# Chunkwise mLSTM cell into a leaky-ReLU feed-forward: one row order of w_in on both partition halves, quarter 2 converted earlier, first feed-forward chunk by token halves

## The chip, the cores and the metric

The kernel runs on one core of one Trainium2 chip. A core has five engines that run side by side, each working through its own instructions in order: TensorE (PE in the profile; PEld is its weight load), VectorE (DVE), ScalarE (ACT), GpSimd (POOL) and SyncE (SP), which here only issues transfers. The metric is the device time of one execution in microseconds. A change is called faster, the same or slower by comparing medians of interleaved runs.

## The reference

Inputs: q, k, v and o_gate of shape (4, 8, 768, 40), i_gate and f_gate of shape (4, 8, 768), and two weight matrices, w_in (320, 2048) and w_out (2048, 320). The weights are float64 in memory, the rest float32. Two blocks follow one another:

```python
for t in range(S):                       # S = 768, per batch and head
    m_new  = max(f[t] + m, i[t])
    f_stab = exp(f[t] + m - m_new);  i_stab = exp(i[t] - m_new);  m = m_new
    C = f_stab * C + i_stab * outer(v[t], k[t])      # 40 x 40
    n = f_stab * n + i_stab * k[t]
    y[t] = sigmoid(o[t]) * (C @ q[t]) / max(abs(n @ q[t]), 1)
x = y laid out as (4 * 768, 320)
out = leaky_relu(x @ w_in, 0.01) @ w_out             # (3072, 320)
```

## The kernel before

The 768 tokens are cut into 6 chunks of 128. A *step* s is one chunk of one of the 4 batch entries: steps 0 to 3 are chunk 0, steps 4 to 7 chunk 1, and so on; all 8 heads go through a step together. The feed-forward (FF) of a chunk takes its 4 x 128 = 512 tokens at once, as `xT` (x transposed). The FF of chunk c - 1 is interleaved on TensorE with the cell steps of chunk c, so that TensorE has matmuls while the cell's chain of other engines runs.

**The rows of w_in and of xT.** Each FF matmul of the first layer uses 64 of the 128 partitions (line 741). The lower half (r = 0) and the upper half (r = 1) compute different output columns, each summing over all five 64-row blocks of w_in, one block per `slot`. `xT` holds the five blocks of x twice, once per half. The table `SLOTS` gives the order of the blocks: 0, 2, 4, 1, 3 in the lower half and 1, 3, 0, 2, 4 in the upper. It decides which rows `load_weights` copies (lines 212 to 217: one transfer of 64 x 256 float64 per slot and half, ten per quarter), which columns `u_x` transposes (line 725), and how `gather_x` reads x back from device memory (two runs per half, four transfers per step).

**Weights.** w_in is loaded and converted in four quarters of 512 columns (`load_weights(0)` to `(3)`, called quarters 1 to 4 here), w_out in eight parts of 256 rows (`load_weights(4)` to `(11)`, w_out parts 0 to 7). A load brings the float64 words into a raw buffer. `narrow_weights` turns them into float32: one Abs on ACT (line 233) and six DVE operations (lines 235, 239, 243, 245, 247, 249). It is a generator, and the code gives it a few operations at a time between other work (`give`, `run(now, ...)`). The raw words of quarters 1 and 2 lie in the not yet used end of `acts`, those of quarters 3 and 4 in a buffer of their own, which w_out parts 2 to 7 use again later.

**The startup, `first_chunk` (lines 833 to 915).** A step of chunk 0 consists of: the mask and the gate sums `ab` (lines 413, 424), the transposes `tkq` (517) copied to `kqT` (522), the exponentials of `w` (441), the scores `sc` (533) multiplied into `w` (537), the state `dC` (545, 553), the values `pa` (620), tanh of the output gate (468), denominators and `x` (611 to 635), and the transposes `xt` (726) copied into `xT` (730, 731). The FF units of chunk 0 are `half(j, h)`: column pair j, token half h. A unit of token half 0 needs `xT` of steps 0 and 1 alone. j = 0 and 1 use quarter 1 of w_in, j = 2 and 3 quarter 2, and so on. Two such units stand inside the startup, `ffs[0]()` and `ffs[1]()`. PSUM buffers for `ab`, for the FF's `ph` and for `po` come from one rotation of four; a unit takes two, and so does a step's `ab`.

**The main loop (lines 936 to 980)** runs the remaining FF units one by one. For c = 1 a list `place` says after which unit each cell unit of chunk 1 comes, `fetch` says where w_out parts are loaded, and `run(now, ...)` how many conversion operations are given per unit. A step of chunk 1 has the transposes `tk` (501) of k and q, copied by ACT (507), the product with the decay `ea` (487), `sd` (591, 596), the masked product (601), and `hN` (646). Then its x is transposed as in chunk 0.

**What sets the order.** On PE, DVE, ACT and POOL the order is the order of the calls. SP is not under that rule: a scheduler orders the transfers it issues. Transfers from SP use eight completion semaphores in turn, so that a transfer is issued only when the eighth before it has landed.

The calls of the startup that the change moves, as they stand before (lines 885 to 892):

```python
        run(prep_exp(2))
        prep_vu(2)
        u_scores(2)
        gates(1)
        u_state(2)
        ffs = ff_units(0)
        ffs[0]()
        gates_exp(1)
```

Of the kernel before, what the change touches and what calls it, by code (L numbers as in the profile page):

```python
# [19 lines left out]
def kernel(  # L20
# [26 lines left out]
    nc = tc.nc  # L47
    B, H, S, D = q.shape
    P = 128
# [5 lines left out]
    DP = 64  # L55
# [11 lines left out]
    KF = Dm // P  # L67
    KR = Dm - KF * P
    KC = Dm // DP
    SLOTS = ([0, 2, 4, 1, 3], [1, 3, 0, 2, 4])  # L70
    assert NB * P == S and NF * P == FF and NF % 4 == 0 and D <= DP and H == 2 * PR and BH <= P
    assert KR == DP and KC == 5 and KC * DP == Dm and GT * 4 <= 2048

# [101 lines left out]
        at = (2 * slot + e) * P  # L175
        return w_in[DP * r : DP * (r + 1), n, at : at + P]

    def run_of(r, at):

        ks = SLOTS[r][at:]  # L180
        return ks[0], next((i for i in range(1, len(ks)) if ks[i] != ks[i - 1] + 2), len(ks))

    HW = 2 * Dm
    wide = moe_w_in.dtype == U64
    raws = {}
# [3 lines left out]
    def load_weights(n):  # L189

        m = n - QN
        if n < QN:
            dst = w_in[:, n, :]
        else:
            dst = w_out[:, 2 * m : 2 * m + 2, :].rearrange("p a d -> p (a d)")
        to = dst
        if wide:
            if n < 2:
                at = NF * GT - 2 * WC * (n + 1)
                raw = acts_l[:, at : at + 2 * WC].bitcast(U64)  # L200
            elif n < QN:
                raw = raw_t[:, WC * (n - 2) : WC * (n - 1)]
            elif m < 2:
                raw = w_out[:].rearrange("p f d -> p (f d)")[:, (2 + m) * WC : (3 + m) * WC].bitcast(U64)
            else:
                at = (4, 0, 1, 2, 3, 4)[m - 2] * HW
                raw = raw_t[:, at : at + HW]
            raws[n] = (raw, dst)
            to = raw
        if n < QN:  # L210
            src = moe_w_in[:, n * QC : (n + 1) * QC].rearrange("(k p) (r c) -> r p k c", p=DP, r=2)
            for slot in range(KC):
                for r in range(2):
                    eng = nc.scalar if n == 0 and r == 1 else nc.sync
                    eng.dma_start(
                        to[DP * r : DP * (r + 1), 2 * P * slot : 2 * P * (slot + 1)], src[r, :, SLOTS[r][slot], :],
                    )
        else:
            rows = moe_w_out[2 * m * P : 2 * (m + 1) * P, :]
            nc.sync.dma_start(to.rearrange("p (a d) -> p a d", d=Dm), rows.rearrange("(a p) d -> p a d", p=P))  # L220
# [107 lines left out]
    def load(s):  # L328
        c, b = divmod(s, B)
        rows = ts(c, P)  # L330
        d = st.setdefault(s, {})
        n = s % NL
        d.update(k=kn[:, n], q=qn[:, n])
        if c == 0:
            d["va"] = S_t[n][:, 1]
            parts = [(d["k"][:, :, :D], k), (d["q"][:, :, :D], q), (d["va"][:, :, :D], v)]
            for dst, src in parts:
                nc.sync.dma_start(dst, src[b, :, rows, :].rearrange("h p d -> p h d"))
            return
        nc.sync.dma_start(d["k"][:, :, :D], k[b, :, rows, :].rearrange("h p d -> p h d"))  # L340
        for u in range(2):
            for i in range(2):
                nc.sync.dma_start(  # L343
                    S_v[n][ts(u, SL), u, :, i, :DB],
                    v[b, :, c * P + u * SL : c * P + (u + 1) * SL, DB * i : DB * (i + 1)].rearrange("h p d -> p h d"),
                )

    def load_o(s):
        c, b = divmod(s, B)
        at = NF * GT - 4 * WC - (s + 1) * Dm  # L350
        st[s]["o"] = acts_l[:, at : at + Dm]
# [253 lines left out]
    def u_state(s):  # L605
        state(s)
        state_copy(s)
# [92 lines left out]
    def gather_x(s):  # L700

        c, b = divmod(s, B)
        if ("xT", c) not in st:
            st["xT", c] = wk.tile([P, KC, GT], F32, name="xT", bufs=1)
        xT = st["xT", c]
        src = x_dr[s].rearrange("(k p) t -> p k t", p=DP)
        for r in range(2):
            at = 0
            while at < KC:
                k0, n = run_of(r, at)  # L710
                nc.sync.dma_start(xT[DP * r : DP * (r + 1), at : at + n, ts(b, P)], src[:, k0 : k0 + 2 * n - 1 : 2, :])
                at += n

    def u_x(s):

        c, b = divmod(s, B)
        d = st[s]
        if b == 0:
            st["xT", c] = wk.tile([P, KC, GT], F32, name="xT", bufs=1)
        xT = st["xT", c]  # L720
        xt = [psc.tile([P, n, P], F32, name=f"xt{n}", tag="c") for n in (KC - 1, 1)]
        for slot in range(KC):
            for r in range(2):
                n, at = divmod(slot, KC - 1)
                kk = SLOTS[r][slot]
                nc.tensor.matmul(  # L726
                    xt[n][DP * r : DP * (r + 1), at, :], lhsT=d["x"][:, ts(kk, DP)], rhs=ident[:], start=True, stop=True,
                )
        tok = ts(b, P)
        nc.scalar.copy(xT[:, : KC - 1, tok], xt[0][:])  # L730
        nc.scalar.copy(xT[:, KC - 1 :, tok], xt[1][:])
        del st[s]


    def ff_units(g):
# [50 lines left out]

        if g == 0:

            ins = [(j, h) for j0 in range(0, NF // 2, 2) for h in range(2) for j in (j0, j0 + 1)]
            return [lambda j=j, h=h: half(j, h) for j, h in ins] + [  # L790
                lambda n=n, m=m: part(n, m) for m in range(4) for n in range(B)
            ]
# [17 lines left out]
    def run(steps, n=None):  # L810

        for _ in range(H if n is None else n):
            next(steps, None)
# [19 lines left out]
    def first_chunk():  # L833

        def give(steps, n=H):
            for _ in range(n):
                next(steps, None)

        load_weights(0)
        load(0)  # L840
        load_fi(1)
        load(1)
        load_o(0)
        load_o(1)
        load(2)
        load(3)
        load_o(2)
        load_o(3)
        load_weights(1)
        load_fi(2)  # L850
        gates(0)
        gates_exp(0)
        spread_mask(0)
        spread_mask(1)
        bu, a, _ = bus[0]
        gates_T(0, bu)
# [60 lines left out]
    E = mybir.EngineType  # L917
    with tc.manual_schedule(engines={E.PE, E.DVE, E.Activation, E.Pool}):
        ffs = first_chunk()
        for s in (B, B + 1):  # L920
            load_weights(s - B + 2)
            feed(s)
            spread_q(s)
            for i in range(1, 3):
                load_late(s, i)
# [3 lines left out]
            feed(s)  # L929


        ffs = ffs[2:]
        fetch = {4: (3, 4), 8: (5, 6), 13: (7,)}
        place = (6, 8, 10, 11, 12, 13, 15, 17, 20, 21, 23, 25, 27)
        now = (None for n in range(2, QN + NF // 2) for _ in narrow_weights(n))
        for c in range(1, NB + 1):
            if c > 1:
# [4 lines left out]
            waiting = []  # L942
            for i in range(n_ff):
                if c == 1:
                    run(now, 2 if i < 10 else 3 if i < 14 else 4)
                    for n in fetch.get(i, ()):
                        load_weights(QN + n)
                    if i == 4:
# [63 lines left out]
```

## Time and profile before

| | |
|---|---|
| median of 3 runs | 547.21 us (546.39 to 547.61) |
| the profiled execution | 546.91 us, of which the profiled span 545.1 us |
| busy: PE, DVE, ACT, POOL | 521.4, 239.0, 156.5, 109.6 us |
| granted TensorE clock, mean | 0.987 |
| first-layer matmuls (line 741) | 1120, 219.4 us |
| second-layer matmuls (line 776) | 768, 215.0 us |

The two FF layers are 80% of the span. DVE, ACT and POOL do most of their work in the first quarter, where the weights are converted beside chunks 0 and 1. An engine's busy time over the whole span therefore says little about the startup; it has to be read stretch by stretch. Positions in the span are given as "at 85.9", in microseconds from its start.

### The profile page before, as it was taken

The numbers are of one execution on the slowest core, as the hardware profiler recorded it, in microseconds if no ns is written. First come the engines' busy times: TensorE is split into PE (matmuls) and PEld (weight loads), VectorE is DVE, ScalarE is ACT, GpSimd is POOL, SyncE is SP. The second block draws the span as 40 slices with busy tenths as digits, with TensorE's granted clock in tenths as the row PEclk, the third lists the DMA queues.
The fourth block names the chain that finished last, engine by engine and source line by source line (L and its number), as shares of the span: only waits on it lengthen the run. The fifth ranks groups of instructions, "written<-read, shape, count | busy, mean of one in ns | idle before, by whom it ended". The sixth has DMA issues, their size and how long they took to land.

```text
span 545.1 us, 11870 instructions
## 1 busy us (share of the span) xinstructions
PE 521.4 (96%) x4776; PEld 333.9 (61%) x4776; DVE 239.0 (44%) x424; ACT 156.5 (29%) x427; POOL 109.6 (20%) x141
## 2 busy tenths in 40 slices
PE   5989895998999999999999999999999999999997
PEld 4767784766755567745567645577654577644675
DVE  4648998799416444226435135525035432000000
ACT  4364643542234412033321034220033300022100
POOL 3425514050203321203332103333002200000000
PEclk9998998898999999999999999999999999999999
DMA  9956687987425555554555655556541121100000
GB/s 160 149 164 148 156 204 198 189 178 139 112 54 125 117 128 119 149 122 110 120 136 128 150 122 105 114 135 140 132 97 56 45 84 35 45 1 0 13 12 24
DMA packets 165814, 60.16 MB, mean 110 GB/s; under 512 B 128960, under 2 KB 156032, under 8 KB 165760
## 3 DMA queue, kind: packets, MB, share of 16 engines
q1 hardware_dynamic: 165264, 58.73, 47.9%
q8 instruction: 37, 0.61, 0.5%
q10 hardware_dynamic: 496, 0.69, 0.4%
q14 instruction: 17, 0.14, 0.1%
HBM read 52.66 MB, written 6.72 MB: 109 GB/s over the span
## 4 chain that ended last, share of the span: by engine, by line
PE 81%; DVE 6%; DMA 4%; issue 4%; SPq 3%; ACT 2%; POOL 1%; ACTq 0%; DVEq 0%; POOLq 0%
PE po L776 36%; PE ph L741 33%; PE pT L676 3%; PE sd L591 2%; DMA acts<-in_moe_w_in_dram 1%; DVE qn L487 1%; PE xt L726 1%; PE sc L533 1%; SPq L343 1%; DMA raw<-in_moe_w_out_dram 1%; PE sd L596 1%; ACT kqT L507 1%; SPq L397 1%; DVE w_out L243 1%; PE tkq L517 1%
## 5 line engine op out<-in xcount | busy, mean ns | idle before, releaser
L741 PE MATMUL ph<-xT,w_in 64*128 64x512 f32 (+1 forms) x1120 | 219.4, 540 | 2.1 <-ACT acts L749 2.0
L776 PE MATMUL po<-w_out,acts 128*128 128x320 f32 x768 | 215.0, 438 | 0.0
L776 PEld LDWEIGHTS po<-w_out,acts 128*128 128x128 f32 x768 | 144.8, 191 | 61.0 <-issue 3.2
L741 PEld LDWEIGHTS ph<-xT,w_in 64*128 64x128 f32 x1120 | 108.4, 190 | 93.0 <-issue 84.5
L749 ACT ACTIVATE acts<-ph 128x512 f32<-128x512 f32 (+1 forms) x112 | 53.9, 534 | 143.3 <-PE ph L741 143.2
L601 DVE TENSOR_TENSOR qn<-w,sd 64x512 f32<-64x512 f32 x40 | 27.4, 685 | 130.1 <-PE sd L596 95.2
L565 POOL TENSOR_TENSOR S<-S,f 40x336 f32<-40x336 f32 x36 | 29.7, 824 | 208.1 <-PE pT L676 153.0
L441 ACT ACTIVATE w<-w,gT 128x64 f32<-128x64 f32 x160 | 42.5, 340 | 6.1 <-POOL w L432 5.7
L487 DVE TENSOR_TENSOR qn<-kqT,ea 64x512 f32<-64x512 f32 (+1 forms) x40 | 30.2, 756 | 6.4 <-ACT kqT L507 5.1
L784 ACT COPY hn<-po 128x320 f32<-128x320 f32 x12 | 5.1, 426 | 87.7 <-PE po L776 87.7
L784 ACT COPY y<-po 128x320 f32<-128x320 f32 x12 | 5.1, 426 | 85.1 <-PE po L776 85.1
L690 POOL TENSOR_TENSOR xb<-xb,den 128x320 f32<-128x320 f32 x16 | 11.7, 728 | 87.4 <-DVE xb L687 87.4
L683 DVE STREAM_TRANSPOSE hb<-pT 128x512 f32<-128x512 f32 x16 | 11.5, 717 | 38.1 <-PE pT L676 38.1
L591 PEld LDWEIGHTS sd<-kqT 40*64 40x64 f32 x640 | 20.2, 135 | 12.3 <-issue 10.4
L432 POOL TENSOR_TENSOR w<-w,i 128x512 f32<-128x512 f32 x20 | 27.4, 1372 | 0.5 <-DMA w<-a_dr 0.5
L591 PE MATMUL sd<-kqT 40*64 40x64 f32 x640 | 23.0, 221 | 0.0
L676 PEld LDWEIGHTS pT<-qn,S 128*64 128x64 f32 x512 | 16.2, 138 | 10.5 <-issue 6.9
L694 DVE STREAM_TRANSPOSE x<-xb 128x512 f32<-128x512 f32 x16 | 17.7, 1107 | 7.7 <-POOL xb L690 7.7
L481 DVE STREAM_TRANSPOSE kqT<-rb 128x512 f32<-128x512 f32 x32 | 20.6, 679 | 0.0
L596 PE MATMUL sd<-S,vu 64*40 64x42 f32 x576 | 20.4, 214 | 0.0
L461 POOL TENSOR_TENSOR vu<-kn,gT 128x320 f32<-128x320 f32 x20 | 17.9, 896 | 3.5 <-DMA kn<-in_k_dram 2.0
L569 DVE TENSOR_TENSOR S<-S,sd 40x336 f32<-40x336 f32 x36 | 18.1, 503 | 0.9
(118 smaller groups left out, 354.4 us busy)
## 6 DMA issues: line engine op xcount, KB each, us to landing
ea<-a_dr SPq DMA_DIRECT2D x40, 128.0 KB
w<-a_dr SPq DMA_DIRECT2D x40, 128.0 KB
rb<-in_k_dram SPq DMA_DIRECT2D x64, 80.0 KB
rb<-in_q_dram SPq DMA_DIRECT2D x64, 80.0 KB
rb<-in_o_gate_dram SPq DMA_DIRECT2D x64, 80.0 KB
kn<-in_k_dram SPq DMA_DIRECT2D x24, 160.0 KB
raw<-in_moe_w_out_dram SPq DMA_DIRECT2D x6, 640.0 KB
S<-in_v_dram SPq DMA_DIRECT2D x80, 40.0 KB
```

Of the source, the lines that this page charges most:

```text
L432: nc.gpsimd.tensor_tensor(w, w, cm2.unsqueeze(1).to_broadcast([P, H, SL]), op=ALU.add)
L441: yield nc.scalar.activation(w[:, h, :], of, AF.Exp, bias=gT[c][:, 0, bh : bh + 1], scale=1.0)
L481: nc.vector.transpose(d["kqT"][:, i].rearrange("p (h t n) -> p h n t", n=TS, t=QW), raw_blocks(s, i, QW).rearrange("p (h n) d -> p h n d", ...
L487: nc.vector.tensor_tensor(mixed(s)[rows, 1 - r], d["kqT"][rows, 1].rearrange("p (h t) -> p h t", t=SL), d["ea"][rows], op=ALU.mult,)
L565: nc.gpsimd.tensor_tensor(new, old, g, op=ALU.mult)
L591: nc.tensor.matmul(bank[1 - u][toks, h, :], lhsT=kqT[rows, 0, ts(h, SL)], rhs=kqT[rows, 1, ts(h, SL)], start=True, stop=True,)
L596: nc.tensor.matmul(dC[u][:, h].rearrange("p k d -> p (k d)"), lhsT=d["ku"][toks, h], rhs=S_v[s % NL][toks, u, h, :, :V1], start=True, stop ...
L601: nc.vector.tensor_tensor(mixed(s)[toks, u], w[toks], bank[1 - u][toks], op=ALU.mult)
L676: nc.tensor.matmul(pT[DP * r : DP * (r + 1), j * P + u * SL : j * P + (u + 1) * SL], lhsT=S[:, u, h, :], rhs=m[:, u, h, :], start=True, st ...
L741: nc.tensor.matmul(ph[r][:, cols], lhsT=w_row(r, slot, j), rhs=xT[DP * r : DP * (r + 1), slot, cols], start=(slot == 0), stop=(slot == KC ...
L749: nc.scalar.activation(acts[:, f, cols], ph[r][:, cols], AF.Prelu, alpha=0.01)
L776: nc.tensor.matmul(po[n][:], lhsT=acts[:, f, ts(n, P)], rhs=w_out[:, f, :], start=(f == 0), stop=(f == NF - 1),)
```

## The change

- `SLOTS` and `run_of` go. Both partition halves take the five row blocks in the order 0 to 4. A quarter of w_in is loaded with one transfer per half (64 x 5 x 256 float64) in place of five. `gather_x` reads x with one transfer per half in place of two. `u_x` transposes the blocks in that order.
- The output gates of steps 0 to 3 are loaded into `w_out[:, s]` in place of a part of `acts`.
- Loads of the startup are called in another order: quarter 2 comes before the loads of step 2, quarter 3 after those of step 3, before anything of chunk 1.
- In `first_chunk`, quarter 1 is converted in one piece earlier; `ab` of step 2 moves behind the state of step 1; the gates of chunk 1 and the conversion of quarter 2 move between steps 1 and 2; four FF units stand in the startup in place of two.
- The first four FF units are (0, 0), (1, 0), (2, 0), (3, 0), all of token half 0, and then (0, 1) to (3, 1). Before, the order was (0, 0), (1, 0), (0, 1), (1, 1), and so on by pairs.
- In the main loop the positions in `fetch` and `place` are two lower, as two units fewer are left, and the number of conversion operations per unit is changed at its start.

```diff
-    SLOTS = ([0, 2, 4, 1, 3], [1, 3, 0, 2, 4])
...
-            for slot in range(KC):
-                for r in range(2):
-                    eng = nc.scalar if n == 0 and r == 1 else nc.sync
-                    eng.dma_start(
-                        to[DP * r : DP * (r + 1), 2 * P * slot : 2 * P * (slot + 1)], src[r, :, SLOTS[r][slot], :],
-                    )
+            for r in range(2):
+                eng = nc.scalar if n == 0 and r == 1 else nc.sync
+                eng.dma_start(to[DP * r : DP * (r + 1), :].rearrange("p (k c) -> p k c", k=KC), src[r])
...
-        at = NF * GT - 4 * WC - (s + 1) * Dm
-        st[s]["o"] = acts_l[:, at : at + Dm]
+        st[s]["o"] = w_out[:, s]
...
         for r in range(2):
-            at = 0
-            while at < KC:
-                k0, n = run_of(r, at)
-                nc.sync.dma_start(xT[DP * r : DP * (r + 1), at : at + n, ts(b, P)], src[:, k0 : k0 + 2 * n - 1 : 2, :])
-                at += n
+            nc.sync.dma_start(xT[DP * r : DP * (r + 1), :, ts(b, P)], src)
...
-            ins = [(j, h) for j0 in range(0, NF // 2, 2) for h in range(2) for j in (j0, j0 + 1)]
+            ins = [(j, h) for h in range(2) for j in range(4)]
+            ins += [(j, h) for j0 in range(4, NF // 2, 2) for h in range(2) for j in (j0, j0 + 1)]
...
         load_o(1)
+        load_weights(1)
         load(2)
+        load_o(2)
         load(3)
-        load_o(2)
         load_o(3)
-        load_weights(1)
+        load_weights(2)
         load_fi(2)
...
         u_transpose(1)
-        spread_mask(2)
-        spread_first(2, a)
-        give(w0, 1)
+        give(w0)
         u_values(0)
...
         u_state(1)
+        spread_mask(2)
+        spread_first(2, a)
         u_values(1)
         prep_o(1)
         gate(1)
-        give(w0)
-        u_transpose(2)
+        gates(1)
         u_x(0)
         u_x(1)
+        give(w1, 1)
         run(prep_exp(2))
-        prep_vu(2)
-        u_scores(2)
-        gates(1)
-        u_state(2)
+        gates_exp(1)
+        give(w1)
         ffs = ff_units(0)
         ffs[0]()
-        gates_exp(1)
+        ffs[1]()
+        prep_vu(2)
+        u_transpose(2)
         spread_mask(3)
         spread_first(3, a)
+        u_scores(2)
+        u_state(2)
+        ffs[2]()
         u_transpose(3)
         run(prep_exp(3))
         prep_vu(3)
-        u_scores(3)
         u_values(2)
         prep_o(2)
         gate(2)
+        u_scores(3)
         u_state(3)
-        give(w1, 2)
-        ffs[1]()
+        ffs[3]()
         u_values(3)
         prep_o(3)
         gate(3)
-        give(w1, 2)
         u_x(2)
         u_x(3)
-        give(w1)
         u_gates(1)
...
         for s in (B, B + 1):
-            load_weights(s - B + 2)
+            if s > B:
+                load_weights(3)
             feed(s)
...
-        ffs = ffs[2:]
-        fetch = {4: (3, 4), 8: (5, 6), 13: (7,)}
-        place = (6, 8, 10, 11, 12, 13, 15, 17, 20, 21, 23, 25, 27)
+        ffs = ffs[4:]
+        fetch = {2: (3, 4), 6: (5, 6), 11: (7,)}
+        place = (4, 6, 8, 9, 10, 11, 13, 15, 18, 19, 21, 23, 25)
...
-                    run(now, 2 if i < 10 else 3 if i < 14 else 4)
+                    run(now, 3 if i < 3 else 2 if i < 8 else 3 if i < 12 else 4)
```

More of the change, by code (lines that the diff above doesn't have):

```diff
@@ L176, in w_row @@
         return w_in[DP * r : DP * (r + 1), n, at : at + P]
-    def run_of(r, at):
-        ks = SLOTS[r][at:]
-        return ks[0], next((i for i in range(1, len(ks)) if ks[i] != ks[i - 1] + 2), len(ks))
     HW = 2 * Dm
@@ L724, in u_x @@
                 n, at = divmod(slot, KC - 1)
-                kk = SLOTS[r][slot]
                 nc.tensor.matmul(
-                    xt[n][DP * r : DP * (r + 1), at, :], lhsT=d["x"][:, ts(kk, DP)], rhs=ident[:], start=True, stop=True,
+                    xt[n][DP * r : DP * (r + 1), at, :], lhsT=d["x"][:, ts(slot, DP)], rhs=ident[:], start=True, stop=True,
                 )
@@ L944 @@
                 if c == 1:
-                    run(now, 2 if i < 10 else 3 if i < 14 else 4)
+                    run(now, 3 if i < 3 else 2 if i < 8 else 3 if i < 12 else 4)
                     for n in fetch.get(i, ()):
                         load_weights(QN + n)
-                    if i == 4:
+                    if i == 2:
                         prep_mask(B)
```

## The prediction

> **What bounds the kernel now.** I read the page's busy line first, then busy time by stretch, TensorE's waits, and the order of time around the largest wait. From the page:
>
> ```profile
> PE 521.4 (96%) x4776; PEld 333.9 (61%) x4776; DVE 239.0 (44%) x424; ACT 156.5 (29%) x427; POOL 109.6 (20%) x141
> ```
>
> TensorE is the bound; at most 545.1 - 521.4 = 23.7 us is idle. Where it lies, by stretch (length, busy time by engine, granted clock, DMA share, GB/s):
>
> ```profile
> 0.00:30.35 30.35, 22.55 (x418) 18.28 (x418) 16.33 (x38) 12.05 (x31) 14.00 (x30) 1.00 1.01 152
> 30.35:53.84 23.49, 20.92 (x331) 17.66 (x332) 14.77 (x32) 13.66 (x38) 6.84 (x16) 0.93 0.60 158
> 53.84:85.10 31.26, 29.01 (x489) 24.81 (x487) 30.48 (x39) 18.12 (x51) 13.21 (x10) 1.00 0.74 170
> 85.10:98.16 13.06, 7.42 (x120) 6.07 (x119) 7.64 (x15) 4.56 (x12) 4.44 (x5) 0.74 0.88 261
> 98.16:122.67 24.51, 24.16 (x316) 17.53 (x314) 23.61 (x36) 11.50 (x32) 7.22 (x6) 1.00 0.85 164
> 142.50:200.00 57.50, 57.50 (x520) 31.76 (x521) 23.55 (x42) 19.43 (x55) 9.91 (x12) 1.00 0.45 102
> ```
>
> After 142.5 TensorE never rests: only a shift of what comes before can change the end. From 53.84 (where quarter 3's conversion starts on DVE) to 85.1 and from 98.16 to 122.67 DVE is full too (30.48 of 31.26, 23.61 of 24.51). Between lies a hole, 85.1 to 98.16, where every engine idles and the clock falls to 0.74. TensorE's waits after 50, and the order of time in the hole (start, duration, queue or engine):
>
> ```profile
> PE tk L501 <- DMA rb<-in_q_dram: 3.2, 1, 3.2
> PE hN L646 <- DVE qn L601: 2.5, 2, 1.5
> PE hN L646 <- DVE S L569: 2.0, 3, 0.9
> PE ph L741 <- ACT acts L749: 2.0, 2, 1.6
> ```
>
> ```profile
> 85.93 1.73 SPq L220 DMA_DIRECT2D raw<-in_moe_w_out_dram  x2
> 87.76 0.41 SPq L366 DMA_DIRECT2D rb<-in_q_dram  x1
> 95.76 2.37 ACT L507 COPY kqT<-tk 40x512 f32<-40x512 f32 x4 [8.45 <-issue]
> 98.16 1.41 DVE L487 TENSOR_TENSOR qn<-kqT,ea 40x512 f32<-40x512 f32 x2 [5.09 <-ACT kqT L507]
> ```
>
> q of step 6 is issued at 87.76, behind two w_out transfers, because SP is late. tk, ACT (8.45 us idle) and DVE (5.09 us) wait for it in turn.
>
> **The change, part by part.**
>
> *Transfers of w_in.* SP spends 3.10 + 7.63 + 7.10 + 6.83 = 24.7 us on 35 issues (the timeline's rows of line 215). Seven remain; at 0.60 (median there) to 0.91 us (a w_out issue, 1.82 for two) they take 4.2 to 6.4. SP gains some 19 us. The bytes are the same.
>
> *First quarter.* Today it lands at 9.42, k of step 0 about 10.4. Now all of it is issued by 2.4 and k and q right behind. At 223 GB/s (5 to 10 us) 1.31 MB takes 5.9, with about 1 to start it lands at 9.3; at 329 GB/s (70 to 75 us) at 7.4; at the 152 GB/s of the first 30 us, k and q among them, at 12.0. I take 9.0, near the 223 of the same place. ACT's Abs, exp and copy (4.4 us) then let sc of step 0 start at 13.6 in place of 13.86; tkq, which follows `ab` at 10.2, allows no less. So 0.3 gained; ends: 0.4 gained, 2.5 lost.
>
> [...]
>
> *The rest of the startup*, by rows of the same work before (lines numbered as before; quarters 1 to 4, steps from 0; sc(1) is step 1's sc). `ab` of step 2 (0.97 + 1.15) leaves the path of kqT(1): sc(1) starts at 19.6 (before 21.9), pa(1) ends 24.4, DVE's x(1) 25.5, POOL 26.7 (1.15, between its 0.72 and 1.92 rows), xt(1) starts 26.7 in place of 29.04, xT is ready 28.7. Up to here 2.3 us are gained. Now two more FF halves come in:
> - half 0: 28.7 to 31.1 (2.36). Half 1 takes the PSUM buffers of ab(2), freed by exp(2), which on ACT stands behind quarter 2's Abs: 28.7 + 1.45 + 2.19 = 32.3; it ends 34.6. A new wait of 1.2; behind it on TensorE stand tkq(2) and ab(3), for which ACT's kqT(2) waits.
> - tkq(2) 35.8, ab(3) 37.5, sc(2) 38.8, dC 39.3; half 2 to 41.5 (quarter 2, six DVE operations of 7.1 us from 30.1, is done at 37.2); tkq(3) 42.7, pa(2) 43.9, sc(3) 45.0.
> - exp(3) ends 46.1; half 3 waits 0.6 for its buffers, with pa(3) behind it: 46.1 to 48.4. tanh(2) is queued behind exp(3) on ACT, so x(2) and with it the product of scores(3) are late: 48.4; pa(3) 49.6, x(3) 51.6, xt(3) 52.9, xT 53.6.
>
> The FF goes on at 53.6 with four halves done (before 50.20 with two; a half is 2.25): tk(4) at 53.6 + 4.5 = 58.1, before 59.03. But Abs of quarter 3 stands behind xT(3) on ACT, 53.6 to 55.0, so DVE starts quarter 3 at 55.0, in place of 53.84, though it idled from 37 to 53. DVE is full from there: 1.2 us late, less one 0.49 conversion (line 235) that the new counts put behind step 4's product: 0.7 late up to hN(5), at 91.0 where it was 90.3.
>
> *The hole.* SP of the changed kernel waits for the gates of chunk 1, which ACT has ready at about 33.5, after exp(2); the loads of steps 4 and 5 stand behind, and nobody needs them before 57. Then 25 issues of about 0.6 go out to q and o of step 5 by 49 (before 65). The w_out parts 3 and 4 need raw space that quarter 3 frees at about 66; q(6) follows at 68, and landing 7.8 later (87.76 to about 95.5 today, where tk's wait ends) makes 76, 15 us before tk(6). That needs no luck. tk(6) 91.0 to 92.1, kqT 94.5 (2.37), DVE's line 487 at 94.5 in place of 98.16: 3.7 us gained. TensorE gains 95.6 - 92.1 = 3.5 and the slow clock's share, so DVE, full from here, sets the gain. What was second is late next: hN(7) still waits for DVE (1.1 today, about the same or 1 more).
>
> *Edits at no cost.* Half as many gathers (64 to 32) leave from SP after 142.5, under a TensorE that has no wait there; if that cover went, 0.6 us an issue. o in w_out: same bytes; rows 0 to 3 are converted after 67, o is read by 50. Row order: same 1120 matmuls on the same partitions. No row prices a different pairing of blocks, but every form of line 741 costs the same per column (2.25 for 20 of 256, 4.49 for 20 of 512), so I take zero; 0.2% of 219 us either way is 0.4.
>
> **The sum** against the profiled execution: 546.91 - 3.7 = 543.2. That execution lies 0.3 below the median, so 547.21 - 3.7 = 543.5. The gain is 58.7 minus the start of quarter 3's conversion: each us in the startup counts in full.
>
> **The rivals.**
> - *The startup is late, slower.* Place: halves 1 and 3, waiting for exp(2) and exp(3), with DVE idle meanwhile. For it: DVE is busy for 1.32 of 5 us in 35 to 40 even today, and the clock after that was 0.66 (40 to 45; half 1 took 3.74 in place of 2.43). Two such (2.6), 1.5 for the first quarter and 1 for x(1)'s POOL product at 1.92: conversion starts at 60.1. It decides from 59.8 (0.2% slower); 547.21 + 1.4 = 548.6. Against: all of these together are needed, and I took none at its fast end.
> - *The hole moves.* q(6) is early, but hN(6) or the w_out parts wait in its place. For it: DVE's 23.61 of 24.51. Then the 0.7 late stays: 547.9. Against: DVE would have to find 3.7 us more work, and the work is the same.
> - *More than I count.* Startup at its fast ends (x(1) at 0.72, less late k) starts conversion at 52.5 to 53, and the dips at 40 to 45, 90 to 100 go (1.3 each on one unit): 7 to 8 us, 539.7. For it: five windows of 5 us at a clock near 0.66. Against: DVE, not the clock, is full on both sides of the hole.
>
> [...]
>
> **How the numbers follow.** Gain of 1.1 to 6 (mine): 0.52. More: 0.20. Within 0.2%, which is 1.1 us and about what a measurement can tell: 0.11 (the moved hole, or a startup 3 late). Slower: 0.17. So faster 0.72. The range leaves out half of the largest gains and half of the losses: 539 to 548.6. My own case alone: 541.2 to 546.1.
>
> **What would show it.** Quarter 3's Abs behind xT(3) and the DVE operation after it at 55 (53 to 57); tk(4) at 58; rb from in_q of step 6 issued near 68, and no wait of tk for it; the 85 to 98 stretch with DVE nearly full; line 487 of step 6 near 94.5; line 741 at 219 us or less. I am wrong if TensorE shows a new wait over 2 us at ph or xt before 55, if conversion of quarter 3 starts after 58, or if the stretch after 142 is no longer full.

## The result and the profile after

No change that can be measured: 547.34 us (545.49 to 550.15, 20 runs) against 547.71 us before (546.30 to 549.66, 20 runs), a ratio of 0.9998 with an interval of 0.9983 to 1.0012. Two later comparisons gave 1.0011 [0.9987, 1.0035] and 1.0011 [0.9989, 1.0033]. The prediction was 543.5 us. The profiled execution took 550.02 us, with a span of 548.2.

The changed kernel's lines are 9 to 15 lower than before: 224 is the Abs, 226 to 240 the DVE conversion, 477 the product with the decay, 491 tk, 591 the masked product, 726 the FF's first layer. In the experiments that follow the same lines stand up to 5 lower in the file.

Busy time by stretch of the changed kernel, with the columns of the table before; the cuts are at the same events (first FF unit, where the table before cuts 1.5 us ahead of it, start of quarter 3's conversion, start and end of the hole):

```profile
0.00:34.36 34.36, 26.12 (x352) 21.81 (x352) 19.17 (x45) 11.53 (x30) 11.55 (x29) 1.00 1.04 154
34.36:59.71 25.35, 23.42 (x412) 19.69 (x414) 13.52 (x24) 14.45 (x41) 5.76 (x13) 1.00 1.02 168
59.71:90.78 31.07, 28.17 (x468) 23.85 (x466) 28.57 (x37) 18.16 (x51) 13.38 (x14) 0.89 0.77 190
90.78:101.12 10.34, 8.30 (x124) 7.06 (x122) 7.18 (x15) 4.02 (x9) 3.88 (x5) 0.68 0.73 194
101.12:125.78 24.66, 24.22 (x316) 17.61 (x314) 23.72 (x37) 12.76 (x36) 7.29 (x7) 0.99 0.82 154
147.00:204.50 57.50, 57.50 (x521) 31.52 (x519) 23.54 (x42) 18.84 (x53) 9.90 (x12) 1.00 0.45 103
```

After 147 TensorE is full, as before. Line 726 takes 220.2 us (219.4 before), but from step 7's masked product to the end this execution takes 422.4 us, as before, so neither the row order nor the gathers show a cost there. The hole is shorter, 10.3 us in place of 13.1, but it ends 3 us later than before: the startup in front of it is longer. TensorE's waits and the rows around the hole (start, duration, engine or queue) in the same execution:

```profile
PE ph L726 <- DVE w_in L240: 2.9, 1, 2.9
PE hN L636 <- DVE qn L591: 2.3, 2, 1.2
PE tkq L507 <- DMA kn<-in_k_dram: 1.1, 1, 1.1
```

```profile
82.86 1.05 SPq L211 DMA_DIRECT2D raw<-in_moe_w_out_dram  x2
84.00 0.42 SPq L356 DMA_DIRECT2D rb<-in_q_dram  x1
98.73 2.37 ACT L497 COPY kqT<-tk 40x512 f32<-40x512 f32 x4 [5.28 <-issue]
101.12 1.62 DVE L477 TENSOR_TENSOR qn<-kqT,ea 40x512 f32<-40x512 f32 x2 [2.83 <-ACT kqT L497]
```

tk no longer waits for q of step 6, as forecast, though q is issued at 84.0 and not near 68. Two waits of more than 1 us are new: tkq of step 0 for k, and the FF for quarter 3. The start of the chain:

```profile
3.68 6.72 SPq L329 DMA_DIRECT2D S<-in_v_dram  x1
11.42 1.36 ACT L224 ACTIVATE w_in<-acts 128x1280 f32<-128x1280 f32 x1 [6.40 <-DMA acts<-in_moe_w_in_dram]
12.19 1.13 PE L507 MATMUL tkq<-ident,kn 64*64 64x64 f32 x32 [1.14 <-DMA kn<-in_k_dram]
15.85 2.08 PE L523 MATMUL sc<-kqT 40*128 40x128 f32 x16 [1.32 <-ACT kqT L512]
```

Quarter 1 lands at 11.4 (before 9.4), k is there at 12.2 (10.45), and sc of step 0 starts at 15.85 (13.86). A second loss of this execution is that small matmuls stay slow until about 34; before, and in the third execution of the changed kernel below, they are fast from about 20. The same rows in the first and the third execution:

```profile
28.25 1.94 PE L610 MATMUL pa<-S,w 128*64 128x41 f32 x32
34.36 2.00 PE L726 MATMUL ph<-xT,w_in 64*128 64x256 f32 x16 [0.47 <-ACT xT L715]
```

```profile
24.53 1.13 PE L610 MATMUL pa<-S,w 128*64 128x41 f32 x32
30.68 5.65 PE L726 MATMUL ph<-xT,w_in 64*128 64x256 f32 x36 [0.38 <-ACT xT L715]
```

The milestones of the executions that the rest speaks of (start, us; rows of the timelines). "Pieces" is the changed kernel with quarter 1 in five transfers per half, "order only" the changed kernel with ten transfers for every quarter:

| | before | changed, 1st | changed, 3rd | pieces, 1st | pieces, 2nd | order only |
|---|---|---|---|---|---|---|
| Abs of quarter 1 | 9.42 | 11.42 | 10.82 | 9.70 | 9.62 | 9.96 |
| sc of step 0 | 13.86 | 15.85 | 15.31 | 14.24 | 14.13 | 14.53 |
| first FF unit | 31.81 | 34.36 | 30.68 | 32.89 | 28.64 | 29.19 |
| conversion of quarter 3 | 53.84 | 59.71 | 56.17 | 58.22 | 54.17 | 54.55 |
| tk(4) | 59.04 | 62.94 | 59.42 | 61.44 | 57.41 | 57.78 |
| masked product, step 5 | 87.16 | 92.84 | 89.34 | 91.37 | 87.86 | 87.63 |
| decay product, step 6 | 98.16 | 101.12 | 97.28 | 99.48 | 96.04 | 95.25 |
| masked product, step 7 | 122.67 | 125.78 | 122.15 | 124.17 | 120.70 | 120.41 |
| span | 545.1 | 548.2 | 545.4 | 546.6 | 543.2 | 542.9 |

From step 7's masked product to the end all of them take 422.4 to 422.5 us, except the third execution of the changed kernel with 423.3. "Changed, 1st" and "pieces, 1st" are the executions with the slow matmuls up to 32 to 34; the other four are compared with one another below.

### The profile page after: what moved, and what is told of

The parts are those of the page before. It is cut to its first block, busy times and chain, and to the rows that moved or that the text cites. A ratio compares the mean times of both kernels' runs of the same rounds, so it can differ in the third digit from the quotient of the medians.

```text
span 548.2 us, 11788 instructions
## 1 busy us (share of the span) xinstructions
PE 527.6 (96%) x4776; PEld 339.9 (62%) x4776; DVE 239.0 (44%) x424; ACT 156.2 (28%) x427; POOL 106.3 (19%) x141
## 3 DMA queue, kind: packets, MB, share of 16 engines
HBM read 52.66 MB, written 6.72 MB: 108 GB/s over the span
## 4 chain that ended last, share of the span: by engine, by line
PE 86%; DMA 5%; DVE 2%; ACT 2%; POOL 2%; issue 1%; SPq 1%; ACTq 0%; POOLq 0%; DVEq 0%
PE po L761 37%; PE ph L726 35%; PE pT L666 3%; PE sd L581 3%; PE xt L711 2%; DMA acts<-in_moe_w_in_dram 2%; DMA raw<-in_moe_w_out_dram 1%; DMA w_out<-in_moe_w_out_dram 1%; PE sc L523 1%; PE pa L610 1%; ACT w L431 1%; PE tkq L507 1%; DMA w<-a_dr 1%; PE sd L586 1%; PE hN L636 1%
## 5 line engine op out<-in xcount | busy, mean ns | idle before, releaser
L726 PE MATMUL ph<-xT,w_in 64*128 64x512 f32 (+1 forms) x1120 | 220.2, 543 | 4.2 <-DVE w_in L240 2.9
L581 PEld LDWEIGHTS sd<-kqT 40*64 40x64 f32 x640 | 20.9, 139 | 12.6 <-issue 10.7
L586 PEld LDWEIGHTS sd<-S,vu 64*40 64x40 f32 x576 | 18.6, 114 | 0.0
```

The lines of the kernel that those rows point to most:

```text
L581: nc.tensor.matmul(bank[1 - u][toks, h, :], lhsT=kqT[rows, 0, ts(h, SL)], rhs=kqT[rows, 1, ts(h, SL)], start=True, stop=True,)
L586: nc.tensor.matmul(dC[u][:, h].rearrange("p k d -> p (k d)"), lhsT=d["ku"][toks, h], rhs=S_v[s % NL][toks, u, h, :, :V1], start=True, stop ...
L726: nc.tensor.matmul(ph[r][:, cols], lhsT=w_row(r, slot, j), rhs=xT[DP * r : DP * (r + 1), slot, cols], start=(slot == 0), stop=(slot == KC ...
```

## The experiments

Times are medians against runs of the kernel before on the same chip.

**The two parts alone.** The kernel before with the natural row order, two transfers per quarter and two per gather, its order of calls kept:

```diff
-            for slot in range(KC):
-                for r in range(2):
...
+            for r in range(2):
+                eng = nc.scalar if n == 0 and r == 1 else nc.sync
+                eng.dma_start(to[DP * r : DP * (r + 1), :].rearrange("p (k c) -> p k c", k=KC), src[r])
```

> The kernel before, with only the row order and the transfers changed (two per quarter, two per gather); the old order of calls, four units in pairs, output gates in acts. Theory A: the first scores start 2 us late (15.9), and SP, with 35 issues less, issues q of step 6 before 87.8; the wait of 3.2 us at tk shrinks; net 545 to 548. Theory B (transfers gain, order loses): 3.7 us faster than before, near 544. A third view, that DMA and not SP's issuing was the limit of the loads: q of step 6 is hardly earlier than 87.8, the wait stays, and the time is 548 to 550.

547.31 us, ratio 1.0009 [0.9990, 1.0028]. Quarter 1 lands at 10.93, and tk(6) still waits 2.71 us for q, which SP issues at 86.70 in place of 87.76. SP has 28 issues fewer, and q gains one microsecond.

And the changed kernel with all quarters in ten transfers:

```diff
-            for r in range(2):
-                eng = nc.scalar if n == 0 and r == 1 else nc.sync
-                eng.dma_start(to[DP * r : DP * (r + 1), :].rearrange("p (k c) -> p k c", k=KC), src[r])
+            for slot in range(KC):
+                for r in range(2):
+                    eng = nc.scalar if n == 0 and r == 1 else nc.sync
+                    eng.dma_start(to[DP * r : DP * (r + 1), 2 * P * slot : 2 * P * (slot + 1)], src[r, :, slot, :])
```

> The changed kernel with ten transfers per quarter for all four quarters (five for each half, natural row order); calls in the new order. Theory A: the startup is as in the run with a first quarter in pieces (scores at 13.9), SP has 28 issues more, some 18 us of SP time, so loads of steps 5 to 7 are later and the hole at tk of step 6 is at least as long as before; 546 to 549. Theory B: 548 to 551, slower than both, because it has the new order's waits without the transfers' gain. If the number of transfers does not matter after quarter 1, it equals the run with a first quarter in pieces within 1 us.

545.34 us, ratio 0.9961 [0.9937, 0.9985]: some 2.1 us faster than before. Quarter 3's conversion starts at 54.55 (the prediction had 55.0), and q of step 6 is issued at 84.01, exactly where the changed kernel issues it with 28 transfers fewer:

```profile
82.87 1.05 SPq L212 DMA_DIRECT2D raw<-in_moe_w_out_dram  x2
84.01 0.42 SPq L357 DMA_DIRECT2D rb<-in_q_dram  x1
95.25 1.86 DVE L478 TENSOR_TENSOR qn<-kqT,ea 40x512 f32<-40x512 f32 x2 [1.63 <-ACT kqT L498]
```

So the gain is the order's, the long transfers bring none, and the two together lose it. (The 84.0 of the changed kernel is from its execution with the slow startup; in its two others q of step 6 goes out at 82.69 and 82.78, so the 28 issues are worth up to 1.3 us there, not 18.)

**Quarter 1 alone in pieces.** The changed kernel, with the five transfers per half for n = 0 only:

```diff
-                eng.dma_start(to[DP * r : DP * (r + 1), :].rearrange("p (k c) -> p k c", k=KC), src[r])
+                if n > 0:
+                    eng.dma_start(to[DP * r : DP * (r + 1), :].rearrange("p (k c) -> p k c", k=KC), src[r])
+            for slot in range(KC if n == 0 else 0):
+                for r in range(2):
+                    eng = nc.scalar if r == 1 else nc.sync
+                    eng.dma_start(to[DP * r : DP * (r + 1), 2 * P * slot : 2 * P * (slot + 1)], src[r, :, slot, :])
```

> The changed kernel, with quarter 1 of w_in in five transfers per half again (natural row order); quarters 2 to 4 keep one per half. Theory A (the long first transfers): the changed kernel's profile has quarter 1 landing at 11.4 in place of 9.4 and the first scores at 15.85 in place of 13.86; with pieces it lands near 9.4, the scores start near 13.9, quarter 3's conversion on DVE starts at 55 to 57 in place of 59.7, and the time falls 2 to 4 us below the changed kernel's 547.3 (543 to 545). Theory B (the new order of calls is what costs): the start moves, but the time stays within 1 us of 547.3, as halves 1 and 3 wait for their PSUM buffers all the same.

545.2 us, ratio 0.9970 [0.9949, 0.9992]. Measured once more:

> The changed kernel with quarter 1 in five transfers per half once more, on the same chip as the two others. Theory (the late landing of quarter 1 took the gain of the order): 545.0 to 545.8 again, 0.25 to 0.45% under the kernel before. Rival (the 0.3% of its first run lay in that chip's or those executions' clock): within 0.15% of the kernel before. If its profiled execution has the fast small matmuls from 20 us on, quarter 3's conversion starts at 54 to 55.5; if the slow ones, at 58 again.

546.24 us against 547.74, ratio 0.9974 [0.9954, 0.9993]. The median is 0.4 above the range of the theory, the ratio in it. Both times the kernel is faster than before, the changed kernel never was; by the ratios the difference between them is 0.24 to 0.41%, or 1.3 to 2.2 us, and only quarter 1 differs. The second execution has the fast matmuls:

```profile
9.62 1.36 ACT L229 ACTIVATE w_in<-acts 128x1280 f32<-128x1280 f32 x1 [3.47 <-DMA acts<-in_moe_w_in_dram]
54.17 0.87 DVE L231 TENSOR_SCALAR w_in<-w_in 128x1280 f32<-128x1280 f32 x1 [0.81 <-ACT w_in L229]
96.04 1.74 DVE L482 TENSOR_TENSOR qn<-kqT,ea 40x512 f32<-40x512 f32 x2 [2.72 <-ACT kqT L502]
```

**The changed kernel again.** Two more executions, to see whether the slow matmuls belong to the change:

> The changed kernel itself once more, for a second profiled execution. If the slow small matmuls up to about 34 us (1.94 and 2.08 us where the kernel before has 1.13 and 1.16 from 20 us on) belong to the change, they are there again and the conversion of quarter 3 starts at 59 to 60. If they differ from execution to execution, they may end at about 20 us, and then it starts at about 56 to 57: 2 us later than with ten transfers for each quarter (54.55), from the landing of quarter 1 alone.

546.58 us (before 546.98). The profiled execution had them again (conversion at 59.30), though six of its ten runs took 545.2 to 547.1 and four 549.4 to 549.9. So once more:

> The changed kernel a third time, for an execution in which TensorE's small matmuls are fast from about 20 us on, as they were in the second execution of the kernel with quarter 1 in five transfers per half (quarter 1 at 9.62, xT(1) 28.64, quarter 3's conversion 54.17, tk(4) 57.41, first product of step 6 at 96.04, step 7 at 120.70). Theory (landing alone separates the two): each of these 1.2 to 1.9 us later: quarter 1 at 10.7 to 11.4, conversion at 55.4 to 56.1, tk(4) at 58.6 to 59.3, step 7 at 121.9 to 122.6 where the kernel before has 122.67. Rival (the changed kernel's executions are always the slow ones, and its time comes from that): slow matmuls to about 34 again, conversion at 59 to 60, step 7 at 125 to 126.

547.42 us (before 547.22). This execution has the fast ones: quarter 1 at 10.82, conversion at 56.17 and tk(4) at 59.42 (0.1 past the range), step 7 at 122.15 (in it). With the startup's clock alike, quarter 1 lands 1.2 us later than in pieces, the first FF unit starts 2.0 later, and step 7's product comes 1.45 later. Some 0.6 of the 2.0 is a pause at `xt` without a releaser (1.08 against 0.45 us), of which more below. The rest is the cost of the long transfer, seen in one chain. The first execution is another 3.6 us behind (125.78 against 122.15); 0.54 of this is there at sc of step 0, the rest comes with the slow matmuls. If the runs of 549.3 us and more are such executions, they are 10 of this kernel's 38.

**Is it k, or quarter 1 itself?** The loads of step 0 ahead of the long transfers, and quarter 1's conversion behind step 0's own work (its other operations follow in three parts, the last ahead of x of step 0):

```diff
-        load_weights(0)
         load(0)
+        load_weights(0)
...
-        give(w0, 5)
         run(prep_exp(0))
         u_transpose(0)
+        give(w0, 1)
```

> The changed kernel with one thing moved: the loads of step 0 (k, q, v) are issued ahead of quarter 1's two long transfers, and quarter 1's Abs and conversion stand behind step 0's own work on ScalarE and VectorE. Theory (what the long transfers cost is k of step 0, which lands behind them): tkq(0) no longer waits for kn and starts at 10.5 to 11 (12.19 in the changed kernel), sc(0) at 13.8 to 14.4 (15.85), and the time falls by 1.5 to 2 us, to about 545.4. Rival (the cost is the landing of quarter 1 itself, 11.42 in place of 9.42, and the conversion behind it): quarter 1 now lands at 12 to 13, and the time stays at 547.3 or gets worse by up to 1 us. Second rival (in the startup TensorE is set by its clock, not by sc(0)): sc(0) moves, the start of quarter 3's conversion does not.

548.6 us, ratio 1.0032 [1.0020, 1.0045]. The rival's case, and more: k comes early, sc(0) starts at 13.62, but quarter 1 lands at 14.7, and its conversion stands in front of x(1) and of the FF:

```profile
13.62 2.08 PE L523 MATMUL sc<-kqT 40*128 40x128 f32 x16 [1.18 <-ACT kqT L512]
28.69 1.61 PE L711 MATMUL xt<-ident,x 128*64 128x128 f32 x20 [2.80 <-POOL x L625]
31.36 2.93 PE L726 MATMUL ph<-xT,w_in 64*128 64x256 f32 x12 [1.06 <-DVE w_in L240]
```

Quarter 3's conversion starts at 57.82, 1.65 later than in the third execution of the changed kernel, though the moved conversion has a part in that. So k alone isn't the cost; whichever of the two comes second is late. (Another 1.4 us of this execution's span lies behind step 7's product, 423.8 in place of 422.4; I have no reading for that.)

**Is it TensorE's clock?** Eleven identity products on TensorE in the pauses before and behind the transposes of step 0, into a PSUM buffer whose content is used up:

```diff
+        warm(5)
         u_transpose(0)
+        warm(6)
```

> The changed kernel with 11 identity products of 128 x 128 on TensorE (5 before and 6 behind the first transposes), into a PSUM tile that is no longer read; nothing else. In the changed kernel's profile TensorE's small matmuls take 1.94 in place of 1.13 until 34 us, though it hardly idles from 16 on. Theory C (the slow clock at the start is a matter of its pauses at 11 to 16): with these filled, pa and sc of steps 0 and 1 take 1.1 to 1.2 from about 20, quarter 3's conversion starts 3 to 4 us earlier, and the time falls to 544 to 546. If the clock is not a matter of those two pauses, the time is 547 to 548.5 (each product costs 0.1 to 0.2).

549.13 us, ratio 1.0040 [1.0019, 1.0062], above both forecasts. The small matmuls are fast from 13.5 on, and nothing is won. The identity products hold tkq back to 13.46 (11.79 in the changed kernel's third execution); the fast rows win that back, so that xt of step 0 starts at 25.58 (25.65); and there TensorE stands for 3 us in the profiled execution, with nothing in the profile to wait for.

```profile
25.58 1.09 PE L714 MATMUL xt<-ident,x 128*64 128x128 f32 x14 [0.41 <-POOL x L628]
29.70 0.55 PE L714 MATMUL xt<-ident,x 128*64 128x128 f32 x6 [3.03 <-issue]
```

**Quarter 3 inside the startup.** The changed kernel's TensorE waits 2.9 us for quarter 3, while DVE was busy for 13.5 of the 25 us before it. Quarter 3's Abs and three DVE operations behind the state of step 2, two behind its gate, the rest behind the gate of step 3. Two things go with it: tanh of step 2 moves ahead of the exponentials of step 3 (`prep_o(2)`), and each of the first three FF units behind the startup is given one conversion operation in place of three:

```diff
         u_state(2)
+        w2 = narrow_weights(2)
+        give(w2, 4)
         ffs[2]()
         u_transpose(3)
+        prep_o(2)
         run(prep_exp(3))
         prep_vu(3)
         u_values(2)
-        prep_o(2)
         gate(2)
+        give(w2, 2)
         u_scores(3)
...
         gate(3)
+        give(w2)
...
-                    run(now, 3 if i < 3 else 2 if i < 8 else 3 if i < 12 else 4)
+                    run(now, 1 if i < 3 else 2 if i < 8 else 3 if i < 12 else 4)
```

> The changed kernel, but quarter 3's Abs and its six VectorE operations stand inside the startup (four behind the state of step 2, two and the rest behind the gates of steps 2 and 3), where VectorE was busy for 13.5 of 25.4 us; in the steps that follow, the first quarters of the FF are given one conversion operation each. Theory (VectorE, full from the start of quarter 3's conversion to the masked product of step 5, 30.5 of 33.1 us, bounds that stretch): conversion of quarter 3 ends at about 55 to 60 in place of 71.3, TensorE's wait of 2.9 us at ph for w_in is gone, the masked product of step 4 comes 5 to 8 us sooner (79.58 in the changed kernel), and the time falls by 3 to 6 us against the changed kernel's 547.3, to 541 to 544. Rival (the startup's chain of masked products, values and x is as tight as VectorE later, so each conversion operation of 0.8 to 1.5 us ahead of a masked product delays the chain): xT(3) comes 2 to 4 us later and the time is within 1 us of the changed kernel's. Second rival (TensorE's own work bounds 60 to 147): only the 2.9 us wait goes, 544 to 545.

546.7 us, ratio 0.9988 [0.9971, 1.0006]: the first rival. Quarter 3 is ready and the wait at ph gone, but the FF behind the startup begins at 59.68, where the changed kernel's second execution, with a first FF unit 4.2 us later, had it at 58.04. With quarter 1 in pieces as well:

> The same, with quarter 1 in five transfers per half in place of one. Theory (the two costs lie one behind the other): another 1.6 to 2 us less than with one transfer per half, so 539.5 to 542. Rival (an earlier startup only lengthens a wait further on, once quarter 3 is converted early): the same time as with one transfer per half, within 0.5 us.

545.46 us, ratio 0.9971 [0.9956, 0.9985]: 1.2 us less than the run before it on the same chip by the medians, 0.9 by the ratios, so between the rival (0.5) and the theory (1.6 to 2), and short of 539.5 to 542. The chain shows a loss: two operations of the conversion ahead of the product of step 3's scores, one of 0.82 us and this one:

```profile
47.77 1.89 DVE L243 SCALAR_TENSOR_TENSOR raw<-raw 128x1280 f32<-128x1280 uint32 x1
49.58 1.27 DVE L532 TENSOR_TENSOR w<-w,sc 128x512 f32<-128x512 f32 x2
68.67 1.41 DVE L482 TENSOR_TENSOR qn<-kqT,ea 40x512 f32<-40x512 f32 x2 [3.54 <-ACT kqT L502]
```

pa(3) waits 2.04 us for that product; tk(4) comes at 65.07, and DVE idles 3.54 us for it. So these two operations were moved behind the gate of step 3:

```diff
         gate(2)
-        give(w2, 2)
         u_scores(3)
```

> Quarter 1 in five transfers per half and quarter 3 converted in the startup, as in the run before it (545.46 us), but the last three conversion operations of quarter 3 stand behind the gates of step 3 and none of them between gate and product of scores of step 3. Theory (those operations, 0.82 + 1.89 us ahead of that product, made pa(3) wait 2.04 us and with it tk(4), which sets step 4 now): the wait of pa(3) for w goes, xT(3) and tk(4) come 1.5 to 2 us sooner (tk(4) 63 to 63.5, was 65.07), and the time is 543.5 to 544.2. Rival (VectorE, 23.2 of 24 us busy from 102 to 126, sets the end whatever comes before): 545 to 546.

543.04 us, ratio 0.9928 [0.9900, 0.9955], from six runs. tk(4) comes at 62.61, 2.5 us sooner, and the time is 0.43% lower by the ratios, 2.4 us: by the times, the theory, slightly exceeded. The profiled execution doesn't show it: it took 545.51 us, as the run before it did (545.47). Its lead is still 2.3 us at step 5's masked product (86.40 against 88.70), and then the wait of the kernel before is back:

```profile
PE tk L496 <- DMA rb<-in_q_dram: 2.7, 1, 2.7
```

q of step 6 is issued at 84.70 (80.77 in the run before), behind two w_out transfers, and step 7's masked product starts at 121.23 (121.27). So in this execution the lead ends at SP, which neither the theory nor the rival named; where the other runs gain 2.4 us isn't shown. Last, tk of step 4 ahead of the first FF unit behind the startup:

```diff
-                    if i == 2:
+                    if i == 0:
                         prep_mask(B)
                         prep_state(B)
                         ahead(B)
+                    if i == 2:
                         load_fi(3)
...
-        place = (4, 6, 8, 9, 10, 11, 13, 15, 18, 19, 21, 23, 25)
+        place = (2, 4, 6, 8, 9, 10, 12, 14, 17, 19, 21, 23, 25)
```

> The same, with TensorE's transposes of step 4 (tk) placed ahead of the first unit of the FF behind the startup in place of the third, and the steps that follow placed one or two units sooner. Theory (with quarter 3 converted, VectorE idles for 4.3 and 3.5 us before step 4 because tk(4) stands behind two FF halves): tk(4) at 56 to 58, the masked queries of step 4 at 61 to 62 in place of 68.7, the masked product of step 7 3 to 5 us sooner than 121.3, time 540.5 to 542.5. Rival (the conversions of w_out, which fill VectorE from 102 to 126, are the bound, or TensorE now waits at ph for the fourth quarter): within 1 us of the kernel without this move.

542.70 us, ratio 0.9925 [0.9898, 0.9951]: within 0.4 us of the run before it, the rival's figure. The milestones did move, tk(4) to 56.34, the masked product of step 7 to 116.78 from 121.23. But the profiled execution of this kernel (541.51) is its fastest and that of the kernel without the move (545.51) its slowest, so the 4.4 us between these two rows are mostly the executions'. Here q of step 6 goes out at 81.42, ahead of the two w_out transfers, and tk waits 0.9 us for it. Busy time from 60 to 95 here:

```profile
60.00:95.00 35.00, 32.73 (x602) 28.24 (x600) 33.33 (x47) 21.40 (x64) 16.92 (x15) 1.00 0.74 181
```

DVE is full again, 33.33 of 35 (27.47 without the move), with work that stood later before. Either of these two versions takes about 0.7% less than the kernel before, with which the changed kernel agrees to about 0.1%.

## Why the prediction was wrong

**First quarter: the step that failed.** It took 9.0 for the landing from the trace's 223 GB/s and had sc(0) 0.3 us earlier. Quarter 1 lands at 10.8 (10.7 and 11.4 in the other two executions) and sc(0) is 1.4 to 2 us later than before; the slow end was 2.5. The rate came from a stretch in which ten pieces were under way and SP issued k, q and v of step 0 only at 5.98, 7.03 and 7.47. With one transfer per half the first bytes come slower (81 GB/s against 153 with pieces from 2 to 4 us, 215 against 279 from 6 to 8), and k, q and v are issued at 2.41, 3.06 and 3.68, so that quarter 1 is under way beside them from then on. How the 1.2 us divide between the size of the transfers and the earlier small loads isn't shown; with k, q and v ahead of it quarter 1 landed at 14.7. Rates by 2 us of the third execution of the changed kernel, and of the second with pieces (last column GB/s, before it the DMA share):

```profile
2.00:4.00 2.00, 0.00 (x0) 0.00 (x0) 1.29 (x5) 1.17 (x2) 1.77 (x5) 1.00 0.45 81
6.00:8.00 2.00, 2.00 (x15) 1.42 (x15) 0.22 (x1) 0.00 (x0) 0.00 (x0) 1.00 1.08 215
```

```profile
2.00:4.00 2.00, 0.00 (x0) 0.00 (x0) 1.34 (x6) 1.16 (x2) 1.77 (x5) 1.00 0.51 153
6.00:8.00 2.00, 2.00 (x17) 1.47 (x17) 0.23 (x1) 0.16 (x1) 0.00 (x0) 1.00 0.98 279
```

That tkq follows `ab` fell with it: k of step 0, issued at 2.41 behind SP's half, is there only at 12.2 and 11.8 in the first and third execution of the changed kernel, and tkq waits 1.1 and 1.2 us for it. Per half, one transfer of 640 KB landed at 10.8 (third execution), five of 128 KB at 9.6 (second with pieces).

**Transfers of w_in: the mechanism was wrong, though the wait went.** SP's 19 us were to bring q(5) to 49 and q(6) to 68. q(5) is issued at 63.84 (before 64.53) and q(6) at 84.0 in the first execution, 82.7 and 82.8 in the others; with the 28 issues back it is 84.01. SP did not spend its time on issues; it stands in them. One transfer of v holds it for 6.72 us behind quarter 1, and the four of step 4 and the four of step 5 for 6.34 and 6.70 us, at 39 and 54, where the DMA engines are full (share 1.02 from 34 to 60; before, from 30 to 54, 0.60). Those of steps 6 and 7, another 5.93 and 3.84 us, stand ahead of q(6) as well. q(6) comes 3.8 us sooner in the first execution; 2 of these are the four transfers of gates (`a_dr` and `fi`) that stood ahead of it from 83.9 to 85.9 and now stand behind it. That was just enough. (Before, tk's wait ended at 93.75, not at 95.5, so q took 6.0 us to land and not 7.8; nothing hung on it.)

**The rest of the startup: right.** Four FF units instead of two, half 1 waiting 0.8 for its buffers (1.2 predicted), pa(2) and x behind them, quarter 3's Abs behind xT(3): with pieces or ten transfers the conversion starts at 54.17 and 54.55, where the sum has 55.0, and tk(4) at 57.41 and 57.78 (58.1). DVE is full from there: 33.1 to 33.7 us from that start to step 5's masked product, 32.9 predicted.

**The hole: shorter, but less than forecast.** From step 5's masked product to step 6's decay product it was 11.0 us, and 6.6 were predicted. It is 7.9 in the third execution (8.2 with pieces, 7.6 with ten transfers). In the third and with pieces the clock there is 0.79, and tk keeps TensorE busy for 1.9 and 1.8 us in place of 1.1; with ten transfers the clock is 1.00, but tk waits 0.71 us for q, the 84 in place of 68.

**The sum, put right** with the third execution's terms: 3.7, less 1.2 (conversion at 56.17, not 55.0), 0.3 (DVE's stretch) and 1.3 (the hole) is 0.9 us, the 98.16 - 97.28 of that execution. Of this 0.4 goes between steps 6 and 7, and 0.8 behind step 7, where the kernel's two other executions lose nothing. So nothing is left in it. The rule that the gain is 58.7 less the start of the conversion was too kind throughout: 4.15 by it with ten transfers, about 2.1 measured.

**The rivals.** The late startup had its place right in part: the conversion starts late in every execution of the changed kernel, 56.2 to 59.7. But it was put down to halves 1 and 3, which wait as counted; the delay enters at step 0, and in two executions at the slow matmuls that follow it. The hole did not move on to hN(6); in the last but one experiment it came back at its old place, tk(6) waiting for q. "More than I count" did not come. The dips of the clock that it priced at 1.3 each (the trace before has four windows of 5 us near 0.66, not five) were small: the granted clock is 1.00 from 34 to 60 in the first execution and 0.94 from 31 to 56 in the third.

## What to carry to other kernels

A transfer at the head of a chain is priced by its landing and by what is under way beside it, not by the issues that it saves: here quarter 1 landed at 10.8, and at 14.7 with k, q and v ahead of it; cutting the first load into pieces won 1.3 to 2.2 us, and merging the others won nothing that the times show. Before costing freed issue time as a gain, look whether the queue's long rows are issues or stalls while the DMA is full: 28 issues fewer were to bring q(6) 19 us forward and brought 0 to 1.3. When work is moved into an engine's idle time, look which operation stands directly behind it, and then which wait is next in line: taking two conversion operations from in front of one product brought tk(4) 2.5 us forward, and in the profiled execution the old wait for q took it all again.

## What the runs showed of the hardware

**The small matmuls of the startup become fast at a time that differs from execution to execution.** The same program, the changed kernel, took 1.94 us for pa at 28 in one execution and 1.13 at 24.5 in another, both with little idle time before it. The column of the granted clock prints 1.00 and 0.99 up to the first FF unit and seems to deny this. But the trace keeps the clock as records of a share, 1.0 or 0.5 in this part of the span, and the first of them, a 1.0, starts at 33.1 and 33.0 us in the first and second execution of the changed kernel, at 20.1 in the third, at 31.8 and 18.2 with pieces, at 19.8 before and at 13.8 with the identity products. That is where the small matmuls become fast in each; ahead of its first record the column rests on nothing. In the first execution TensorE is busy for all of the 17.3 us between sc of step 0 and the first record, in the third for all of 4.8 us, so the length of unbroken work alone does not set the time. The first FF unit starts 3.7 us later in the first execution, of which 0.5 was there at sc of step 0. Three of the fourteen profiled executions are of the late kind, and all three are of the changed kernel or of the one with quarter 1 in pieces; whether the change makes them likelier isn't shown.

**TensorE pauses behind the same number of instructions, with no wait that the profile shows.** In six executions with fast matmuls TensorE pauses at `xt` without a releaser: 0.45, 0.50, 0.77, 1.05, 1.08 and, with the identity products, 3.03 us. In each, 348 weight loads and 347 or 348 matmul rows of TensorE stand before the pause; with 22 matmul rows added ahead it comes 21 `xt` rows sooner. With the semaphore and drain instructions that the trace lists for TensorE, 705 instructions stand before it each time. Between 16 and 60 us every other pause over 0.15 us that matmul rows show without a releaser stands at such a place too, in all fourteen executions: 0.19 to 1.23 us behind the 1217th, 512 later, in seven executions, and 0.21 us behind the 449th, 256 earlier, in the one with the identity products. Three executions with fast matmuls and the same program up to there (ten transfers, k ahead, step 4 early) have no pause behind the 705th. A 16 KB packet of the queue that the profile calls `instruction` is under way shortly before (it begins between 24 and 27), while the packets of the other transfers take 138 to 148% of the 16 engines' time, in the 1 or 2 us in which it begins (five of the six executions). The row of the third execution of the changed kernel:

```profile
29.74 0.57 PE L711 MATMUL xt<-ident,x 128*64 128x128 f32 x5 [1.08 <-issue]
```

The three places are 256 and 512 instructions apart. Why TensorE pauses there, and whether the packet or the full DMA engines have a part in it, isn't shown: no run changed either of them alone.
